# A two-layer spectral mixer with an MLP on one core: weight steps after every sequence product and on another engine, matrix loads at other calls, more places for second weights

## The chip, the cores and the metric

The kernel runs on one core of one Trainium2 chip. The metric is the device time of one execution in microseconds (us), lower is better. Before the change the median of 3 runs is 2772.48 us (2771.77 to 2774.47). TensorE (PE) multiplies, VectorE (DVE), ScalarE (ACT) and GpSimd (POOL) do elementwise work, and SyncE (SP) issues every DMA of this kernel, in the order of the program.

## The reference

The input is x of 2048 tokens by 576. Two layers run one after the other, and each is two residual steps, a Fourier mixing and an MLP:

```python
x = x + _A_ref(_layernorm(x), seq_re, seq_im, hid_re, hid_im)   # layer 1
x = x + _B_ref(_layernorm(x), w1, b1, w2, b2)
x = x + _A_ref(_layernorm(x), seq_re, seq_im, hid_re, hid_im)   # layer 2, same weights
x = x + _B_ref(_layernorm(x), w1, b1, w2, b2)

a = einsum("bsd,ed->bse", x, hid_re); b = einsum("bsd,ed->bse", x, hid_im)     # _A_ref
y = einsum("ts,bse->bte", seq_re, a) - einsum("ts,bse->bte", seq_im, b)
h = gelu(einsum("bsd,df->bsf", layernorm(x), w1) + b1)                          # _B_ref
y = einsum("bsf,fd->bsd", h, w2) + b2
```

The MLP's inner width is 4608. All data are 32-bit floats.

## The kernel before, in words

**Numbers in two parts.** Every matrix operand is kept as a high and a low part (the low part is the value minus its rounded high part), and each product is three passes, high by high, high by low, low by high. The high part is an ACT copy, the low part a subtraction. The products are arranged in a seven-product scheme (`ORDER` gives the order 1, 6, 2, 5, 7, 3, 4), so that sums and differences of operand blocks must be made as well.

**Stages.** The program runs, for each of the two layers: `Sequence.run` (products along the sequence, results to `uv_mid` in memory), then twice (half 0 and half 1 of the tokens) the function `hidden` (products with the hidden matrix, whose parts lie in `dh_parts`, and the normalization) with `mlp` behind it. I call the layers 1 and 2.

**The sequence.** After two first tiles, `run` (L602) goes through 14 tiles of 7 products. Each step makes the low part of the operand two products ahead on DVE (`low`, L556), the high part three ahead on ACT (`high`, L551), the 24 matmuls (`mms`) and the work on the result (`post`, L577). In `post` of product 7, ACT copies the bank, POOL adds (L593) and DVE combines (L594). Once per tile DVE makes two sums for the next tile (`sums`, L544), from blocks whose load is issued when a block of this tile comes free.

**The weight steps.** In layer 1 the first weights w1 must be split once for all later use. The generator `weights` (L247) does this in 126 steps, 7 for each of 18 groups. A step is: two ACT copies into a staging block (`high`, L265), later the subtraction (`low`, L270, at L275) and a store to `w1_parts`; in four steps of seven, POOL also makes the next operand (the `add` and `sub` of L251), and in four a block of raw weights is loaded. Each call of `pump` does one `low` and the next `high`. `run` calls it through `tick(3)`, three times in four products; the first products of the MLP (`inner`, L1003) call `tick(2)`, once in two products, and `load_w` calls it where a group is not made yet. After the 98 sequence products 73 pumps are done, and 55 more steps fall into the first MLP.

**The MLP.** `mlp` (L911) runs 18 times `inner` (7 products each with w1, results through gelu into hidden blocks), and behind each odd and even one a part of `outer` (L1098) for the pair of the step before: products 1, 6, 5, 3 behind the even one, 7, 4, 2 behind the odd. `outer` makes two calls of 12 matmuls for each product. Its second weights w2 come in slots `c2` of 4 x 288 elements: in half 0 two slots and a third that `give1` adds. In layer 1, half 0 (`first`), they are made on the way by `make` (L951): POOL differences, an ACT high part (L957), a DVE low part, and a store to `w2s`; a slot must have been stored before it is written again. In all later halves `load_w` loads them.

**Getting half 1 ready.** In the last `outer` of half 0 (g == 8, 14 calls) each call also does `next(after)`, a step of `Hidden.steps` (L685): it takes the place of Y, loads x, the sequence results `uv_mid` and the nine blocks of `dh_parts` (576 KB each), and turns the first tile on PE. All these loads and those of w2 go through SP's queue, in order.

Of the kernel before, what the change touches and what calls it, by code (L numbers as in the profile page):

```python
# [153 lines left out]
def spectral_mixer(ctx: ExitStack, tc: tile.TileContext, x, dh, c0, cs, w1, b1, w2, b2, out):  # L154
# [38 lines left out]
    def sub(engine, dst, a, b):  # L193
        engine.tensor_tensor(dst, a, b, op=OP.subtract)  # L194
# [46 lines left out]
        nc.scalar.activation(dst, src, AF.Identity, bias=mv[:, 4:5], scale=mv[:, 3:4])  # L241


    made = [0]
    stage, raw = R.alloc(3 * 5 * P, low=True), A.alloc(4 * 3 * P, low=True)

    def weights():  # L247
# [14 lines left out]
        def cut(a):  # L262
            return a.rearrange("p (k f) -> p k f", f=P)
# [6 lines left out]
        def low(n):  # L270

            q, k = divmod(n, 7)
            i, src, then = steps[k]
            t = cut(at(n))
            sub(nc.vector, t[:, 0:5:2], cut(src), t[:, 1:4].bitcast(F32))  # L275
            dma(w1s[q, i - 1], at(n).bitcast(F32))
            if then:
                then()
            if k in (2, 4, 5, 6):
                load(q + 1, (2, 4, 5, 6).index(k))  # L280
            if k == 6:
                made[0] = q + 1
# [32 lines left out]
    class Sequence:  # L315
# [286 lines left out]
        def run(self, hidden):  # L602
# [17 lines left out]
            for n, (t, i) in enumerate(steps):  # L620
                self.load_c()
                if n + 2 < len(steps):
                    self.low(*steps[n + 2])
                if i == 2 and t + 1 < NT:
                    self.sums(t + 1)
                self.load_c()
                if n + 3 < len(steps):
                    self.high(*steps[n + 3])
                self.mms(t, i)
                self.post(t, i)  # L630
                if t == NT - 1:
                    hidden.begin(self, ORDER.index(i))
                tick(3)
            for k in range(2):
                self.L[k].free()
            self.own.close()
# [5 lines left out]
    class Hidden:  # L642
# [41 lines left out]

        def steps(self):  # L685
            self.uvs = Slots(R, 2, 2 * D, Y_AT[0])
            self.X = A.place(X_AT[1], NT * DH)
            self.places = [R.place(Y_AT[0] + 4 * D + k * 2 * D, 2 * D) for k in range(KH)]

            def load_d(k):  # L690
                b = self.places[k].at
                self.load_d(k, Block(R, b, D), Block(R, b + D, D))

            self.load(0)
            load_d(0)
            yield
            self.load(1)
            load_d(1)
            for k in range(KH):
                yield  # L700
                if k + 2 < KH:
                    load_d(k + 2)
                self.high_d(k)
                if k:
                    self.low_d(k - 1)
            yield
            self.low_d(KH - 1)
            drain(self.turn(0, R.place(UT_AT[1][0], 2 * KH * P)))
            self.load_uv(2)
            yield  # L710
# [200 lines left out]
    def mlp(hid, store, first, after):  # L911
# [186 lines left out]
        def outer(g, i, side):  # L1098
            for jj in range(2):
# [14 lines left out]
                work(slot[0] % 3 < 2 or g >= last - 1)  # L1114
                slot[0] += 1
                advance()
                if g == last:
                    next(after, None)
                to = goal[i][:, 2 * jj:2 * jj + 2]
                if i == 6 and g == 0:  # L1120
# [24 lines left out]
        for g in range(NG + 1):  # L1145
            at[0] = 0
            if first and g:
                due.extend(make(g - 1))
            if g == NG:
                work(99)  # L1150
                c1.close()
                hs.close()
                Y.free()
            for f in range(2):
                if g < NG:
                    for _ in inner(2 * g + f, None if g or f else 1):
                        pass
                if g:
                    advance(6 + 15 * f)
                    at[0] = 7 + 15 * f  # L1160
                    slot[0] = 0
                    for i in OUTER[f]:
                        outer(g - 1, i, 1 - f)
# [81 lines left out]
```

## Time and profile before

| what | before |
|---|---|
| median of 3 runs | 2772.48 us |
| the profiled execution | 2771.1 us, of which its span is 2769.3 us |
| PE busy | 2684.4 us (97%) |
| DVE, ACT, POOL busy | 1756.6, 1087.4, 791.9 us |
| DMA moved | 543.74 MB, mean 196 GB/s |

The profile is of one execution. Its lists give, for an engine, the time that it stood idle and what ended that idle time; `A` and `R` are the two large on-chip buffers (plain, and rounded for matmul), `bank` is the accumulator memory, and `w_parts`, `dh_parts`, `uv_mid`, `x_mid` are tensors in memory. In a list by time the columns are start, length, engine, line, operation, operands, count, and in brackets the idle time before and what ended it. Lines 191 and 194 are the helpers `add` and `sub`, line 201 is `mm`, line 188 is `dma`, so a group is told apart by its operands and shape. By time, layer 1's sequence lies at about 12 to 376 us, its half 0 until 908, its half 1 until about 1390; layer 2's sequence until about 1770, half 0 until 2271, half 1 to the end.

### The profile page before, as it was taken

How to read it: one execution, taken by the hardware profiler on the slowest of the kernel's cores; microseconds unless marked ns; L12 is line 12 of the kernel's file. 1: busy time of each engine (PE TensorE's matmuls, PEld its weight loads, DVE VectorE, ACT ScalarE, POOL GpSimd, SP SyncE). 2: the span in 40 equal slices, each digit the busy share in tenths (PEclk: the TensorE clock that was granted, in tenths of full speed). 3: DMA queues.
4: the chain of work that ended last, by engine and by line, in shares of the span. 5: the costliest groups of instructions: out<-in, count | busy, mean ns of one | idle time of the engine just before them, and what ended most of it. 6: DMA issues, size and time to landing. Idle time of an engine off the chain costs nothing.

```text
span 2769.3 us, 45580 instructions
## 1 busy us (share of the span) xinstructions
PE 2684.4 (97%) x17596; PEld 2513.2 (91%) x17596; DVE 1756.6 (63%) x2566; ACT 1087.4 (39%) x1850; POOL 791.9 (29%) x762
## 2 busy tenths in 40 slices
PE   7999999999999999999989999999999999999999
PEld 7999998788888988989889999998999989998988
DVE  8788866777776465555577666555555544655555
ACT  6555544544443243333254333334333313433331
POOL 5222223544534332222251000042222224221222
PEclk9999999999999999999999999999999999999999
DMA  5666675777776546666553333526666663566664
GB/s 198 240 222 223 231 257 172 268 263 271 263 262 216 216 152 195 192 196 192 168 206 119 124 126 125 187 98 208 194 195 192 189 247 132 185 194 195 191 197 152
DMA packets 208712, 543.74 MB, mean 196 GB/s; under 512 B 21985, under 2 KB 56801, under 8 KB 208353
## 3 DMA queue, kind: packets, MB, share of 16 engines
q1 hardware_dynamic: 208496, 540.84, 58.7%
q8 instruction: 139, 2.28, 0.3%
q14 instruction: 77, 0.62, 0.1%
HBM read 428.69 MB, written 114.72 MB: 196 GB/s over the span
## 4 chain that ended last, share of the span: by engine, by line
PE 69%; DVE 5%; issue 3%; DMA 3%; POOL 2%; ACT 1%; SPq 0%; POOLq 0%; DVEq 0%; ACTq 0%
PE bank L201 68%; DVE R L194 2%; DMA R<-w_parts 1%; DVE A L191 1%; POOL A L194 1%; DMA A<-x_mid 1%; PE bank L764 1%; POOL R L194 1%; DMA w_parts<-R 0%; DVE bank L191 0%; DVE A L194 0%; DVE moments L216 0%; DVE moments L231 0%; ACT R L957 0%; ACT R L1073 0%
## 5 line engine op out<-in xcount | busy, mean ns | idle before, releaser
L201 PE MATMUL bank<-R 128*128 128x288 f32 (+2 forms) x16972 | 2624.9, 316 | 72.3 <-DVE A L191 23.3
L201 PEld LDWEIGHTS bank<-R 128*128 128x128 f32 x16972 | 2447.5, 189 | 240.9 <-DVE A L191 30.3
L191 DVE TENSOR_TENSOR A<-bank,A 128x576 f32<-128x576 f32 (+3 forms) x808 | 567.4, 710 | 613.5 <-PE bank L201 533.6
L194 POOL TENSOR_TENSOR R<-A,R 128x512 fp32r<-128x512 f32 x288 | 374.3, 1310 | 981.5 <-ACT R L1073 948.6
L194 DVE TENSOR_TENSOR R<-A,R 128x1024 fp32r<-128x1024 f32 (+4 forms) x449 | 447.3, 1024 | 44.7 <-ACT R L554 25.4
L191 POOL TENSOR_TENSOR A<-A 128x576 f32<-128x576 f32 (+2 forms) x102 | 131.1, 1287 | 639.0 <-ACT A L592 349.6
L1013 ACT ACTIVATE bank<-bank,b1t 128x512 f32<-128x512 f32 (+1 forms) x224 | 144.8, 646 | 373.8 <-DVE bank L191 253.6
L194 DVE TENSOR_TENSOR R<-bank,R 128x512 fp32r<-128x512 f32 (+4 forms) x408 | 251.6, 636 | 59.7 <-ACT R L197 50.2
L1073 ACT ACTIVATE R<-A 128x512 fp32r<-128x512 f32 x288 | 176.2, 628 | 276.4 <-DVE A L194 117.3
L554 ACT ACTIVATE R<-A 128x1024 fp32r<-128x1024 f32 x196 | 204.0, 1054 | 135.4 <-DVE A L194 105.5
L191 DVE TENSOR_TENSOR bank<-bank,A 128x512 f32<-128x512 f32 (+1 forms) x228 | 152.2, 670 | 152.1 <-PE bank L201 151.7
L194 POOL TENSOR_TENSOR A<-A 128x288 f32<-128x288 f32 (+2 forms) x170 | 200.6, 1193 | 154.9 <-DVE R L194 83.9
L197 ACT ACTIVATE R<-bank 128x512 fp32r<-128x512 f32 (+2 forms) x160 | 74.1, 514 | 185.6 <-PE bank L764 129.3
L1073 ACT ACTIVATE R<-bank 128x512 fp32r<-128x512 f32 x216 | 120.7, 595 | 32.0 <-PE bank L201 32.0
L194 DVE TENSOR_TENSOR A<-A 128x1024 f32<-128x1024 f32 (+2 forms) x116 | 127.7, 1106 | 4.3 <-ACT A L241 1.2
L1040 ACT ACTIVATE A<-bank 128x512 f32<-128x512 f32 (+1 forms) x76 | 43.7, 575 | 211.6 <-PE bank L201 208.9
L241 ACT ACTIVATE A<-A,moments 128x576 f32<-128x576 f32 x64 | 54.0, 868 | 113.0 <-POOL moments L224 80.7
L194 DVE TENSOR_TENSOR A<-bank,A 128x512 f32<-128x512 f32 x144 | 98.2, 682 | 0.0
L594 DVE SCALAR_TENSOR_TENSOR A<-A 128x288 f32<-128x288 f32 x28 | 18.4, 657 | 88.4 <-POOL A L191 88.4
L1013 ACT ACTIVATE A<-bank,b1t 128x512 f32<-128x512 f32 (+1 forms) x76 | 50.4, 663 | 54.8 <-DVE bank L191 54.8
L268 ACT ACTIVATE R<-A,power,middle 128x128 fp32r<-128x128 f32 x126 | 60.8, 483 | 0.0
L222 POOL TENSOR_TENSOR moments<-moments,power 128x1 f32<-128x1 f32 x32 | 17.6, 551 | 148.3 <-DVE moments L219 148.3
(50 smaller groups left out, 632.4 us busy)
## 6 DMA issues: line engine op xcount, KB each, us to landing
R<-w_parts SPq DMA_DIRECT2D x504, 320.0 KB, 3.3
R<-w_parts SPq DMA_DIRECT2D x189, 576.0 KB, 3.7
A<-in_cs SPq DMA_DIRECT2D x112, 512.0 KB, 4.3
w_parts<-R SPq DMA_DIRECT2D x126, 320.0 KB, 3.7
w_parts<-R SPq DMA_DIRECT2D x63, 576.0 KB, 4.0
uv_mid<-A SPq DMA_DIRECT2D x32, 576.0 KB, 2.8
A<-in_w SPq DMA_DIRECT2D x72, 192.0 KB, 3.8
R<-dh_parts SPq DMA_DIRECT2D x23, 576.0 KB, 10.5
```

The costliest lines, as they stand in the source:

```text
L191: engine.tensor_tensor(dst, a, b, op=op)
L194: engine.tensor_tensor(dst, a, b, op=OP.subtract)
L197: nc.scalar.activation(hi, src, AF.Copy)
L201: nc.tensor.matmul(o, a, b, start=start, stop=stop, skip_group_check=True)
L241: nc.scalar.activation(dst, src, AF.Identity, bias=mv[:, 4:5], scale=mv[:, 3:4])
L268: nc.scalar.activation(t[:, 2], src[:, 1], AF.Identity, bias=power[:, 2:3], scale=middle)
L554: nc.scalar.activation(self.cells[t, i](2, NP, P)[:, 0], self.source(t, i), AF.Copy)
L594: nc.vector.scalar_tensor_tensor(uv[:, 1, 0], p7, -1.0, u, op0=OP.mult, op1=OP.subtract)
L764: nc.tensor.transpose(at, v[:, k], ident)
L1013: nc.scalar.activation(dst, src, AF.Gelu_apprx_tanh, bias=bias(f))
L1040: nc.scalar.activation(up, o, AF.Copy)
L1073: nc.scalar.activation(H[q, k](2, TC)[:, 0], src, AF.Copy)
```

## The change

It has four edits.

1. `weights` subtracts on GpSimd while the first sequence runs, and on VectorE afterwards (`in_sequence`).
2. `run` pumps after every product, 98 times, in place of `tick(3)`.
3. `Hidden.steps` loads the nine matrix blocks one at each of its first nine steps and x behind them, and its steps begin six calls earlier, in `outer(7, ...)` of 7, 4, 2. For that Y and the w1 slots are freed behind the last `inner`, not at the next round.
4. In half 0, `c2` gets a place at R 0 as soon as that is free (in layer 1 when the weight steps are done), and behind the last `inner` two places where w1 lay.

```diff
-    made = [0]
+    made, in_sequence = [0], [True]
...
-            sub(nc.vector, t[:, 0:5:2], cut(src), t[:, 1:4].bitcast(F32))
+            sub(g if in_sequence[0] else nc.vector, t[:, 0:5:2], cut(src), t[:, 1:4].bitcast(F32))
...
-                tick(3)
+                pump()
+            in_sequence[0] = False
...
             self.uvs = Slots(R, 2, 2 * D, Y_AT[0])
-            self.X = A.place(X_AT[1], NT * DH)
             self.places = [R.place(Y_AT[0] + 4 * D + k * 2 * D, 2 * D) for k in range(KH)]
-
-            def load_d(k):
+            self.load_uv(0)
+            for k in range(KH):
                 b = self.places[k].at
                 self.load_d(k, Block(R, b, D), Block(R, b + D, D))
-
+                yield
+                if k == 2:
+                    self.load_uv(1)
+            self.X = A.place(X_AT[1], NT * DH)
             self.load(0)
-            load_d(0)
             yield
             self.load(1)
-            load_d(1)
-            for k in range(KH):
+            for _ in range(6):
                 yield
-                if k + 2 < KH:
-                    load_d(k + 2)
-                self.high_d(k)
-                if k:
-                    self.low_d(k - 1)
-            yield
-            self.low_d(KH - 1)
             drain(self.turn(0, R.place(UT_AT[1][0], 2 * KH * P)))
...
-                if g == last:
+                if g == last or half == 0 and g == last - 1 and side == 0:
                     next(after, None)
...
                 work(99)
-                c1.close()
                 hs.close()
-                Y.free()
+            if half == 0 and len(c2.idle) < 4:
+                more = R.place(0, 4 * DH)
+                if more:
+                    c2.idle.append(more)
...
+                if g == last and f:
+                    c1.close()
+                    Y.free()
+                    if half == 0:
+                        c2.idle += [R.place(C1_AT[0] + k * 4 * DH, 4 * DH) for k in range(2)]
```

**POOL in layer 1's sequence.** These are POOL's rows over one tile and a bit; 128x384 is the operand that a weight step makes, 128x288 is the addition of `post` of product 7. Before:

```order
L191 TENSOR_TENSOR A<-A 128x384
L191 TENSOR_TENSOR A<-A 128x288
L194 TENSOR_TENSOR A<-A 128x384 x3
L191 TENSOR_TENSOR A<-A 128x288
L191 TENSOR_TENSOR A<-A 128x384
```

With the change, where 128x3x128 is the subtraction of a weight step:

```order
L194 TENSOR_TENSOR R<-A,R 128x3x128 x4
L191 TENSOR_TENSOR A<-A 128x384
L194 TENSOR_TENSOR R<-A,R 128x3x128
L194 TENSOR_TENSOR A<-A 128x384
L191 TENSOR_TENSOR A<-A 128x288
L194 TENSOR_TENSOR R<-A,R 128x3x128
L194 TENSOR_TENSOR A<-A 128x384
L194 TENSOR_TENSOR R<-A,R 128x3x128
L194 TENSOR_TENSOR A<-A 128x384
```

Every tile now has seven subtractions, four operands and the addition on POOL, always in the same places: the subtraction of 7's pump stands right behind the addition that DVE waits for. On DVE the rows 128x3x128 are gone from the sequence, and 30 are left in the first MLP.

**SP at the end of half 0, layer 2.** These are the loads of SP's queue; 128x1152 from `w_parts` is one second weight (640 is a first weight, the last ones). Before, from the last first weights to the stores of the result:

```order
L188 DMA R<-w_parts 128x1152 x3
L188 DMA R<-uv_mid 128x1152
L188 DMA A<-x_mid 128x2x288
L188 DMA R<-dh_parts 128x1152
L188 DMA R<-uv_mid 128x1152
L188 DMA A<-x_mid 128x2x288
L188 DMA R<-dh_parts 128x1152
L188 DMA R<-w_parts 128x1152
L188 DMA R<-dh_parts 128x1152 x2
L188 DMA R<-w_parts 128x1152
L188 DMA R<-dh_parts 128x1152 x2
L188 DMA R<-w_parts 128x1152
```

With the change, from the same place:

```order
L188 DMA R<-w_parts 128x1152
L188 DMA R<-uv_mid 128x1152
L188 DMA R<-dh_parts 128x1152
L188 DMA R<-w_parts 128x1152
L188 DMA R<-dh_parts 128x1152
L188 DMA R<-w_parts 128x1152
L188 DMA R<-dh_parts 128x1152
L188 DMA R<-uv_mid 128x1152
L188 DMA R<-dh_parts 128x1152
L188 DMA R<-w_parts 128x1152
L188 DMA R<-dh_parts 128x1152 x2
L188 DMA R<-w_parts 128x1152
```

The second and third row of matrices now stand before second weights that were ahead of all of them, but the whole list begins with `outer(7, ...)` of 7, 4, 2, six calls earlier, and x has moved behind the matrices.

**SP at the end of half 0, layer 1.** Here the second weights are stored. Before:

```order
L188 DMA R<-dh_parts 128x1152 x2
L188 DMA w_parts<-R 128x1152
L188 DMA R<-dh_parts 128x1152 x3
L188 DMA w_parts<-R 128x1152
L188 DMA R<-dh_parts 128x1152 x2
L188 DMA w_parts<-R 128x1152 x2
```

With the change:

```order
L188 DMA R<-dh_parts 128x1152 x3
L188 DMA R<-uv_mid 128x1152
L188 DMA R<-dh_parts 128x1152 x3
L188 DMA w_parts<-R 128x1152 x2
L188 DMA R<-dh_parts 128x1152
L188 DMA w_parts<-R 128x1152
```

Six of the nine matrix loads have moved ahead of all seven stores of the last second weights.

## The prediction

> **What bounds the kernel now.** I read the page first, then busy time by stretch, then what PE waited for in each stretch, then the list by time around the longest waits, and last the groups of VectorE and GpSimd in the two sequences.
>
> ```profile
> span 2769.3 us, 45580 instructions
> PE 2684.4 (97%) x17596; PEld 2513.2 (91%) x17596; DVE 1756.6 (63%) x2566; ACT 1087.4 (39%) x1850; POOL 791.9 (29%) x762
> ```
>
> PE is the bound: 85 us are all that it stands idle, so each edit is worth what it gives back, or takes, there. The stretches are, from the top, layer 1's sequence, the end of its first MLP, its change from half 0 to half 1, layer 2's sequence, and layer 2's change to half 1.
>
> ```profile
> core 0: us, PE busy (x) PEld busy (x) DVE busy (x) ACT busy (x) POOL busy (x), PEclk, DMA share, GB/s
> 100.00:376.00 276.00, 276.00 (x2090) 276.00 (x2089) 229.49 (x251) 151.08 (x271) 67.87 (x49) 1.00 0.68 230
> 836.00:876.00 40.00, 38.94 (x235) 34.72 (x233) 27.82 (x41) 16.07 (x27) 15.67 (x12) 1.00 0.53 184
> 866.00:911.00 45.00, 36.38 (x238) 34.67 (x237) 26.05 (x36) 10.61 (x18) 18.33 (x13) 0.89 0.71 269
> 1500.00:1760.00 260.00, 260.00 (x1969) 260.00 (x1968) 169.66 (x177) 100.92 (x129) 9.71 (x12) 1.00 0.33 117
> 2246.00:2276.00 30.00, 24.10 (x169) 23.40 (x168) 11.15 (x16) 1.26 (x3) 8.98 (x7) 0.94 0.95 365
> ```
>
> In both sequences PE never stops, so there the change can only lose. At the two changes of half PE loses 8.6 of 45 us and 5.9 of 30 us, and the granted clock falls to 0.89 and 0.94: there it can win.
>
> **Layer 1's change of half (more places, earlier loads).** The list by time, SP's, ACT's, DVE's and PE's rows:
>
> ```profile
> 889.20 5.25 SPq L188 DMA_DIRECT2D R<-dh_parts  x3
> 895.54 0.32 SPq L188 DMA_DIRECT2D w_parts<-R  x1
> ...
> 900.63 0.68 ACT L957 ACTIVATE R<-A 128x576 fp32r<-128x576 f32 x1 [5.73 <-DMA w_parts<-R]
> 902.02 1.42 DVE L191 TENSOR_TENSOR A<-bank,A 128x576 f32<-128x576 f32 x2
> 902.91 5.22 PE L201 MATMUL bank<-R 128*128 128x288 f32 x24 [5.96 <-DVE A L191]
> ```
>
> Read it backwards. PE waits 5.96 us for DVE to empty a bank; DVE stood behind a low part; that behind ACT's copy, which waited 5.73 us until the store of a second weight had freed its slot; and the store stood in SP's queue behind matrix loads. With the change `c2` has six places by then (two, `give1`'s, R 0, and two of w1's; the steps are done long before, so R 0 is free), and seven weights are made: six copies find a free place, the seventh that of product 1, whose store is first of all. Six of the nine matrix loads leave the queue earlier, too. So the 5.96 us go. For the speed behind it:
>
> ```profile
> 2258.79 8.04 PE L201 MATMUL bank<-R 128*128 128x288 f32 x48 [4.17 <-DMA R<-w_parts]
> 2267.93 3.44 PE L201 MATMUL bank<-R 128*128 128x288 f32 x24 [1.11 <-DMA R<-w_parts]
> 2272.20 1.86 PE L201 MATMUL bank<-R 128*128 128x288 f32 x12
> ```
>
> 24 matmuls take 3.44 us at full clock and took 5.22 behind the wait, 1.78 more. Together **-7.7**. The short waits at the head of this `outer` (its first weight is made just before it is used) I leave, for their order does not change.
>
> **Layer 2's change of half.** The same rows show its price: 4.17 and 1.11 us of waiting for second weights, and 48 matmuls in 8.04 us where 3.44 + 2 x 1.58 = 6.60 would do (1.58 is 3.44 less 1.86), 1.44. Together 6.7. The weights stood behind matrix loads in a queue that moved 365 GB/s at a share of 0.95. With the change the queue begins six calls, some 6 x 1.6 = 9.6 us, earlier, and one more weight is there when it begins. From there it carries six weights and nine matrices of 0.59 MB, two of `uv_mid` of the same size, and x, 10.6 MB. The last weight is the 16th piece: 9.4 MB / 365 GB/s = 26 us. It is used at the 19th call, 18 x 1.6 = 29 us on; the one before it is the 13th, 21 us, and used at 26. Both come in time by 3 to 5 us, so **-6.7**.
>
> **The first MLP (fewer steps in it).** What PE waited for, first from 676 to 836 us, then from 836 to 876, after the last weight step:
>
> ```profile
> PE bank L201 <- DVE bank L191: 3.3, 4, 0.8
> PE bank L201 <- DVE A L191: 1.8, 3, 0.6
> PE bank L201 <- DMA R<-w_parts: 1.3, 2, 0.7
> ...
> PE bank L201 <- DVE A L191: 1.0, 1, 1.0
> ```
>
> With steps going on, there is a wait in each `inner` (six, 4.6 us; DVE comes late to a bank that the last product needs) and one in each second `outer` (three, 1.8 us). Without them only the one in `outer` is left, with 1.0 us. Now 30 steps are left for this MLP, one in two products, so 60 products, 8.6 of 18 `inner`: they end near 676 us, as I count the `inner` in PE's rows. From there to 836, 6.4 us become 3 x 1.0: **-3.4**. Before 676 the steps stand at the same products as they did, so nothing.
>
> **Layer 1's sequence (a step per product, subtracted by GpSimd).** Groups of DVE and POOL, first from 100 to 376 us, then of DVE in layer 2's stretch, where no step runs; the last number before the idle time is the mean in ns:
>
> ```profile
> L194 DVE TENSOR_TENSOR R<-A,R 128x1024 fp32r<-128x1024 f32 x87 | 111.5, 1284 | 6.1 <-ACT R L554 6.0
> L194 DVE TENSOR_TENSOR A<-A 128x1024 f32<-128x1024 f32 x36 | 48.3, 1341 | 1.2
> L194 DVE TENSOR_TENSOR R<-A,R 128x384 fp32r<-128x384 f32 x65 | 39.5, 608 | 0.6 <-issue 0.6
> L594 DVE SCALAR_TENSOR_TENSOR A<-A 128x288 f32<-128x288 f32 x13 | 10.7, 825 | 26.7 <-POOL A L191 26.7
> L194 POOL TENSOR_TENSOR A<-A 128x384 f32<-128x384 f32 x27 | 40.0, 1480 | 57.7 <-DVE R L194 30.1 <-issue 23.0 <-DMA A<-in_w 4.1
> L191 POOL TENSOR_TENSOR A<-A 128x384 f32<-128x384 f32 x9 | 17.2, 1910 | 97.7 <-DVE R L194 97.7
> ...
> L194 DVE TENSOR_TENSOR R<-A,R 128x1024 fp32r<-128x1024 f32 x82 | 98.9, 1219 | 9.8 <-ACT R L554 9.8
> L594 DVE SCALAR_TENSOR_TENSOR A<-A 128x288 f32<-128x288 f32 x12 | 5.5, 459 | 54.3 <-POOL A L191 54.3
> ```
>
> The same DVE operation is longer where POOL works: 1284 against 1219 ns, 825 against 459. The list by time shows why:
>
> ```profile
> 152.73 1.00 POOL L194 TENSOR_TENSOR A<-A 128x384 f32<-128x384 f32 x1
> 157.88 1.02 POOL L194 TENSOR_TENSOR A<-A 128x384 f32<-128x384 f32 x1 [4.15 <-issue]
> ...
> 152.80 1.25 DVE L594 SCALAR_TENSOR_TENSOR A<-A 128x288 f32<-128x288 f32 x1 [2.06 <-POOL A L191]
> 155.69 1.22 DVE L194 TENSOR_TENSOR A<-A 128x1024 f32<-128x1024 f32 x1
> 157.20 0.55 DVE L194 TENSOR_TENSOR R<-A,R 128x384 fp32r<-128x384 f32 x1
> 158.10 1.88 DVE L194 TENSOR_TENSOR R<-A,R 128x1024 fp32r<-128x1024 f32 x1 [0.35 <-ACT R L554]
> ```
>
> A DVE operation on two on-chip operands that meets a POOL operation ends only when POOL has ended and its own work is done: 1.88 in place of 1.22, 1.25 in place of 0.46. One meeting costs DVE 0.66 to 0.79 us. So what leaves DVE comes back as hold-up. The sum over these 276 us (12.4 tiles of 22.2 us): DVE without steps takes 169.66 / 260 x 276 = 180. Before, 229.5: 65 subtractions of 0.55 are 36, the other 13 are hold-up by 49 POOL operations. After: no subtractions, but 87 of them and 50 operand steps (four in seven) on POOL, 137 operations of 1.00 us beside the 13 additions. At the hold-up of before (13.5 / 49 = 0.28 each) DVE comes to 180 + 38 = 218, and nothing is lost. If each meets DVE, it comes to 180 + 137 x 0.66 = 270, or with 0.79 to 288: 6 below the 276 or 12 above, over 14 tiles nothing or 14 us. I take the row of 0.66, since DVE works nearly without a break then and nearly each meets it; its 6 us are 0.5 us a tile, and the waits that DVE cannot fill (0.35 for ACT above, and the 2.06 where 7's pump now puts a subtraction right behind the addition) take some more than that, an estimate of 0.3 us a tile: **+4**, between 0 and 14.
>
> The other parts cost nothing I can name: ACT has 25 steps of two short copies more, in a stretch where it is busy 151 of 276 us; SP's queue has 25 stores more and the share of the DMA is 0.68; but SP now waits for POOL before it issues a store, and matrix loads for the next tile's sums stand behind it. That is in the 14 us.
>
> On this the Trainium skill has a rule: "SBUF — State Buffer", section "SBUF: two separate sides", says that VectorE operations with two SBUF inputs and GpSimd share a port pair as an exclusive lock, held for the whole instruction. The rows agree in kind (an operation is held up, not slowed), and by 0.66 to 0.79 us, not by the whole 1.00. The skill's "GPSIMD Engine Reference", section "4.1 Engine selection", advises against GpSimd for elementwise work; taken alone, it would make the subtraction 1.00 for 0.55 us and change nothing while PE bounds.
>
> **The sum.** 2769.3 - 7.7 - 6.7 - 3.4 + 4 = 2755.5 us of span. The profiled execution took 2771.1, 1.8 more than its span, and the median 2772.48, 1.4 above that: 2755.5 + 1.8 + 1.4 = **2758.7**.
>
> **Rivals.**
> - *VectorE and GpSimd take turns all through layer 1's sequence, and bound it* (slower). Each of 137 operations would hold DVE up for its whole 1.00 us: 180 + 137 = 317 for 276, over 14 tiles (311 us) +46 in place of +4: 2801. It costs anything from (276 - 180) / 137 = 0.70 us of hold-up on, and the kernel is slower by over 0.2% from 0.86 on. For it speaks that POOL's mean is already 1480 and 1910 ns, waiting its own turn; against it that no quoted DVE operation was held 0.86. Up to 0.86 the gain is only eaten: 2764 to 2778. The skill's lock, held for the whole instruction, would make this 2801.
> - *The loads are late anyway* (layer 2). If the queue moved 300 GB/s, the last weight would land at 31 us, 2 us after its use; with the slower clock behind the wait some 4 of the 6.7 us stay: 2763. For it: four weights and six matrices are now issued in under 10 us.
> - *The stall of layer 1 isn't the slot's.* If ACT's copy would wait for the difference that POOL makes for it as long as for the slot, the 7.7 us stay: 2766. Against it: its row names the store.
>
> **How the numbers follow.** The forecast 0.62 (own range 2752 to 2764); gains eaten by hold-up 0.20; slower by it 0.08; late loads or the stall staying 0.10. The range 2750 to 2776 leaves out the slow end and gains beyond those counted. A run can tell 0.2%, 5.5 us, from no change. Faster by more than that (under 2767): 0.62, most of the last case, and a little of the second, 0.74; within, 0.18; slower, 0.08.
>
> **What would show it.** Right: PE's waits from 676 us on without those of `inner`; no wait over 2 us at either change of half, and the clock near 1 there; in layer 1's sequence PE busy nearly throughout, DVE near 270 of 276 us, its 1024-wide subtraction at a mean of 1.5 to 1.9 us. Wrong: PE idle in layer 1's sequence, ended by DVE, of more than 1 us a tile; or waits for `w_parts` left in layer 2.

## The result, and the profile after

The changed kernel takes 2773.89 us (median of 12 runs, 2770.63 to 2776.7), the kernel before on the same chips 2771.89 (12 runs, 2769.98 to 2774.47): a ratio of 1.0008, interval 1.0000 to 1.0015. No difference that can be told, where I forecast 2758.7.

The page's head, the counterpart of the two lines of before:

```profile
span 2773.3 us, 45524 instructions
...
PE 2689.5 (97%) x17596; PEld 2513.7 (91%) x17596; DVE 1766.4 (64%) x2470; ACT 1085.8 (39%) x1850; POOL 954.4 (34%) x858
```

PE has the same 17596 matmuls and idles 83.8 us (2773.3 - 2689.5) where it idled 84.9: nothing seems to have happened. Cut at marks that both traces have, it is a large gain and a large loss. The marks are the first transposes of `turn` (L764 before, L758 now) of a layer, and the first 256-wide matmul of an MLP:

| stretch of PE's rows, us | before | after | difference | forecast |
|---|---|---|---|---|
| start to layer 1's first transposes | 376.6 | 395.1 | **+18.5** | +4 |
| on to its first MLP | 80.0 | 85.8 | **+5.8** | 0 |
| on to the MLP of its half 1 | 531.9 | 517.5 | **-14.4** | -7.7 - 3.4 |
| on to layer 2's first transposes | 788.5 | 790.0 | +1.5 | 0 |
| on to the MLP of its half 1 | 574.8 | 567.5 | **-7.3** | -6.7 |
| on to the last matmul | 410.8 | 410.7 | -0.1 | 0 |
| sum | 2762.6 | 2766.6 | +4.0 | -13.8 |

The sum is the difference of the two spans, 2773.3 - 2769.3. The first MLP and the ends of the halves gave 21.7 us, more than the 17.8 forecast; layer 1's sequence and what follows it took 24.3. The +1.5 arises where layer 2's sequence begins: between 1380 and 1500 us PE's longest wait is 7.3 us where it was 5.9; why was not followed.

**The ends of the halves.** Busy time by stretch, after, with the same columns as before: layer 1's sequence, layer 1's change of half, layer 2's.

```profile
100.00:376.00 276.00, 268.30 (x1977) 262.46 (x1976) 246.13 (x176) 152.33 (x291) 219.73 (x143) 1.00 0.72 245
...
875.00:920.00 45.00, 40.81 (x260) 37.62 (x259) 30.49 (x43) 13.47 (x23) 17.82 (x13) 0.96 0.87 321
2250.00:2281.00 31.00, 30.29 (x228) 29.78 (x228) 18.02 (x28) 3.79 (x7) 13.71 (x10) 1.00 0.81 318
```

At the changes of half the clock is 0.96 and 1.00 where it was 0.89 and 0.94. What PE waited for, in us, times and longest, before, first from 836 to 911 us, then from 2225 to 2285:

```profile
PE bank L201 <- DVE A L191: 7.6, 4, 6.0
...
PE bank L201 <- DMA R<-w_parts: 5.3, 2, 4.2
```

And after: from 100 to 376, from 376 to 481, from 700 to 855 (the stretch that was 676 to 836), from 855 to 920, and from 2225 to 2290 us:

```profile
PE bank L201 <- DVE R L194: 6.8, 17, 0.7
...
PE bank L201 <- DVE R L194: 6.3, 4, 4.5
...
PE bank L201 <- DMA R<-w_parts: 0.3, 1, 0.3
...
PE bank L201 <- DVE A L191: 3.4, 5, 1.0
...
PE bank L201 <- DVE A L191: 0.7, 1, 0.7
```

The wait of 6.0 us is gone (1.0 is left in its place), and so are the 5.3 for second weights in layer 2. Where layer 1's half 0 got its 14.4 us (14.5 before rounding) shorter is seen by comparing the n-th matmul of PE after with the n-th before. The changed kernel is 24.4 us late at the first matmul of the first MLP, 23.6 late at the matmul that before has at 676 us, 16.6 at 836 and 16.5 at 895, 11.5 behind the long wait, and 9.8 from 920 us on. So the first MLP gave 7.9 us, 7.0 of them from 676 us on (6.1 are waits: 0.3 where 6.4 had been), and the change of half 6.7: 5.0 by the wait, 1.7 by the matmuls behind it, which ran at a higher clock.

**Layer 1's sequence.** PE, busy for all 276.00 us before, is busy for 268.30, in 1977 matmuls where 2090 were done. The waits are small, 17 of at most 0.7 us in this list, and these are all for a DVE low part. The count says more than the busy time: at 276 / 2090 = 0.132 us each, the 113 matmuls that are missing are 14.9 us, while the rows book 7.7 as idle; the rest is in PE rows that have grown longer. A tile takes 23.63 us on the mean where it took 22.21. POOL and DVE by groups in the same stretch, in the form of the prediction's; the first row is POOL's addition before, the others are after:

```profile
L191 POOL TENSOR_TENSOR A<-A 128x288 f32<-128x288 f32 x13 | 11.0, 844 | 51.6 <-ACT A L592 51.6
...
L194 POOL TENSOR_TENSOR R<-A,R 128x384 fp32r<-128x384 f32 x83 | 121.7, 1466 | 54.2 <-ACT R L268 50.5 <-POOL R L194 3.7
L194 POOL TENSOR_TENSOR A<-A 128x384 f32<-128x384 f32 x36 | 61.2, 1700 | 0.9
...
L191 POOL TENSOR_TENSOR A<-A 128x288 f32<-128x288 f32 x12 | 20.6, 1718 | 0.5
...
L194 DVE TENSOR_TENSOR R<-A,R 128x1024 fp32r<-128x1024 f32 x82 | 147.1, 1805 | 8.9 <-ACT R L554 8.4
L194 DVE TENSOR_TENSOR A<-A 128x1024 f32<-128x1024 f32 x36 | 60.8, 1690 | 1.2
```

DVE is as forecast in kind (1805 and 1690 ns for its large operations), and busy for 246 us, not 270: it idles 30 us of 276. POOL is the news: the addition for product 7 has a mean of 1718 ns where it had 844. DVE, ACT and POOL over one tile, chosen from the list by time:

```profile
254.28 1.26 DVE L594 SCALAR_TENSOR_TENSOR A<-A 128x288 f32<-128x288 f32 x1 [0.70 <-POOL A L191]
...
260.57 1.23 DVE L194 TENSOR_TENSOR R<-A,R 128x1024 fp32r<-128x1024 f32 x1 [0.76 <-ACT R L554]
...
263.78 1.92 DVE L194 TENSOR_TENSOR A<-A 128x1024 f32<-128x1024 f32 x1
...
263.07 0.89 SPq L188 DMA_DIRECT2D A<-in_w  x1
265.74 0.33 SPq L188 DMA_DIRECT2D A<-in_cs  x1
266.16 0.38 SPq L188 DMA_DIRECT2D w_parts<-R  x1
266.60 0.43 SPq L188 DMA_DIRECT2D A<-in_w  x1
...
271.64 0.42 ACT L267 ACTIVATE R<-A 128x256 fp32r<-128x256 f32 x1 [2.96 <-DMA A<-in_w]
...
275.23 0.39 ACT L592 ACTIVATE A<-bank 128x288 f32<-128x288 f32 x1
...
272.52 1.19 POOL L194 TENSOR_TENSOR R<-A,R 128x384 fp32r<-128x384 f32 x1 [2.03 <-ACT R L268]
273.68 1.99 POOL L194 TENSOR_TENSOR A<-A 128x384 f32<-128x384 f32 x1
275.70 1.71 POOL L191 TENSOR_TENSOR A<-A 128x288 f32<-128x288 f32 x1
...
277.44 1.25 DVE L594 SCALAR_TENSOR_TENSOR A<-A 128x288 f32<-128x288 f32 x1 [0.70 <-POOL A L191]
```

This is a closed loop, and its turn, 277.44 - 254.28 = 23.16 us, is the tile. DVE combines product 7's result, and comes to the block subtraction that ends at 265.70; SP, which goes by the order of the program, issues nothing from 263.96 until then, when its load of `in_cs` may overwrite that block, and behind it stand a store and the load of a raw weight block, issued at 266.60; ACT stands at the copy of it until 271.64; POOL then does that step's subtraction and operand, 1.19 and 1.99 us, and only behind them the addition for product 7, 1.71 us; then DVE combines again. DVE takes 11.4 us of the turn, SP 0.9, the load 5.0, ACT 0.9 and POOL 4.9. Two lines end at the addition almost together: POOL's operand at 275.67, and ACT's copy of product 7's result (L592), which ACT comes to only behind the weight copies, at 275.62. So by these rows, taking either one away alone would gain little.

### The profile page after: what moved, and what is told of

It reads as the page before. It is cut to its first block, busy times and chain, and to the rows that moved or that the text cites. A ratio compares the mean times of both kernels' runs of the same rounds, so it can differ in the third digit from the quotient of the medians.

```text
span 2773.3 us, 45524 instructions
## 1 busy us (share of the span) xinstructions
PE 2689.5 (97%) x17596; PEld 2513.7 (91%) x17596; DVE 1766.4 (64%) x2470; ACT 1085.8 (39%) x1850; POOL 954.4 (34%) x858
## 4 chain that ended last, share of the span: by engine, by line
PE 73%; DVE 3%; DMA 2%; issue 2%; POOL 1%; ACT 1%; SPq 0%; POOLq 0%; DVEq 0%; ACTq 0%
PE bank L201 72%; DVE R L194 1%; DMA R<-w_parts 1%; POOL A L194 1%; PE bank L758 1%; DVE A L191 1%; POOL R L194 0%; DMA A<-in_cs 0%; DMA w_parts<-R 0%; DMA A<-x_mid 0%; DVE moments L216 0%; DVE A L194 0%; PE bank L828 0%; DVE moments L231 0%; ACT R L483 0%
## 5 line engine op out<-in xcount | busy, mean ns | idle before, releaser
L194 POOL TENSOR_TENSOR R<-A,R 128x512 fp32r<-128x512 f32 (+1 forms) x384 | 519.2, 1361 | 1120.1 <-ACT R L1067 998.1
L194 DVE TENSOR_TENSOR R<-A,R 128x1024 fp32r<-128x1024 f32 (+5 forms) x353 | 430.8, 1239 | 46.2 <-ACT R L554 31.5
L191 POOL TENSOR_TENSOR A<-A 128x576 f32<-128x576 f32 (+2 forms) x102 | 144.5, 1419 | 380.9 <-ACT A L592 298.9
L194 POOL TENSOR_TENSOR A<-A 128x288 f32<-128x288 f32 (+2 forms) x170 | 207.1, 1226 | 107.3 <-DVE R L194 53.1
L194 DVE TENSOR_TENSOR A<-A 128x1024 f32<-128x1024 f32 (+2 forms) x116 | 141.6, 1226 | 4.3 <-ACT A L241 1.3
L267 ACT ACTIVATE R<-A 128x256 fp32r<-128x256 f32 x126 | 51.5, 409 | 64.9 <-DMA A<-in_w 49.2
L594 DVE SCALAR_TENSOR_TENSOR A<-A 128x288 f32<-128x288 f32 x28 | 24.0, 856 | 73.7 <-POOL A L191 73.7
```

The source lines that it names most:

```text
L191: engine.tensor_tensor(dst, a, b, op=op)
L267: nc.scalar.activation(t[:, 1:4:2], src[:, 0:3:2], AF.Copy)
L594: nc.vector.scalar_tensor_tensor(uv[:, 1, 0], p7, -1.0, u, op0=OP.mult, op1=OP.subtract)
```

## Experiments

Each table gives layer 1's first transposes (where the sequence ends), the mean of the 12 tiles behind the first, and the time with its ratio to the kernel before on the same chip. A tile is taken from one copy of product 7's result on ACT to the next.

### One edit at a time

a1 undoes edit 1, a2 edit 2, a3 both (all with the diff's lines), a4 undoes edits 3 and 4, so that only the steps are left.

```diff
 a1: -            sub(g if in_sequence[0] else nc.vector, t[:, 0:5:2], ...
     +            sub(nc.vector, t[:, 0:5:2], ...
 a2: -                pump()
     +                tick(3)
```

> Edit 1 undone: every weight subtraction on VectorE, still a step per product. Theory H (GpSimd's operations hold VectorE up on the chain from product 7 to the low part of the next tile's product 6): 82 subtractions of 0.55 us return to VectorE and 82 hold-ups go; the first hidden product of layer 1 begins near 377 us as before the change (395 with it), tiles of 22.2 us, and the span is 2773.3 less 15 to 22: 2751 to 2758. Rival R (the step rate: two more ACT copies, a store and waits of SP's queue per product): the tiles stay at 23 us or more and the span at 2768 to 2774.

> Edit 2 undone: three steps in four products, subtracted by GpSimd. H: 103 GpSimd operations in place of 142 hold VectorE up, tiles of 22.3 to 22.9 us, so 2 to 10 us of the sequence's 24 stay lost; in the first MLP 55 steps stand again, 3 to 6 us back: span 2757 to 2767. R: tiles of 22.2 us, no loss in the sequence: span 2753 to 2757.

> Edits 1 and 2 undone: only the loads, the earlier steps and the places for second weights. Both theories: the sequence as before the change, the two changes of half as with it (7.7 and 7.3 us less than before), the first MLP's steps as before: span 2753 to 2756. If part of the first MLP's gain comes from the fourth place and not from fewer steps, down to 2750.

> Edits 3 and 4 undone: only GpSimd's subtraction and a step per product. Both theories: the sequence's 24 us lost and 3 to 7 us won in the first MLP, the waits at the changes of half as before: span 2786 to 2792. If the last tile of the sequence loses its 6 us through something that the loads at the ends set off, less than that.

| kernel | subtraction | steps in a tile | transposes at | tile | us | ratio (interval) |
|---|---|---|---|---|---|---|
| before | DVE | 5.25 | 376.6 | 22.21 | | |
| after | POOL | 7 | 395.1 | 23.63 | 2773.89 | 1.0008 (1.0000 to 1.0015) |
| a1 | DVE | 7 | 394.8 | 23.54 | 2777.90 | 1.0012 (1.0003 to 1.0022) |
| a2 | POOL | 5.25 | 378.2 | 22.31 | 2763.52 | 0.9962 (0.9947 to 0.9977) |
| a3 | DVE | 5.25 | 376.6 | 22.21 | 2759.17 | 0.9950 (0.9934 to 0.9967) |
| a4 | POOL | 7 | 394.2 | 23.53 | 2789.38 | 1.0055 (1.0040 to 1.0070) |

The gain of the ends (a3) and the loss of the steps (a4) stand apart: edits 3 and 4 alone give 0.5%, a span of 2757.3 us, a little less gain than the 2753 to 2756 that I expected. The steps are not a sum of two costs: the fourth step in four costs 18.2 us with DVE subtracting and 16.9 with POOL, and POOL's subtraction costs 1.6 with three steps in four and nothing with all. So hold-up of DVE by POOL, on which my forecast rested, can't be the whole: a1 takes POOL's 96 subtractions in the sequence away and loses the same.

### Where the wait is, and where it goes

In a1 ACT waited for raw weights too (19.2 us from 100 to 376), as in the change (37.3). So I tried the group's last three steps in the order 6, 7, 3, which reloads the late block earlier (b1 as the change, b2 with DVE), no reload in the sequence at all (b3), and no steps in the last tile (b4).

```diff
 b1: -                 (7, a21, None), (6, a11, None), (3, a12, None))
     +                 (6, a11, None), (7, a21, None), (3, a12, None))
     ...
     -                load(q + 1, (2, 4, 5, 6).index(k))
     +                load(q + 1, {2: 0, 4: 2, 5: 1, 6: 3}[k])
 b3: -            if k in (2, 4, 5, 6):
     +            if k in (2, 4, 5, 6) and not in_sequence[0]:
 b4:                  if t == NT - 1:
                          hidden.begin(self, ORDER.index(i))
     -                pump()
     +                else:
     +                    pump()
```

> The changed kernel with the last three steps of a weight group in the order 6, 7, 3 in place of 7, 6, 3, so that the raw block a11 is loaded again one step earlier, four pumps before ACT copies it in place of two. Theory W (with a step per product a weight group takes one tile, and ACT, in order, stands before the copy of a raw block that has not landed; the operand copies of the sequence stand behind it): ACT's waits for in_w (37 us from 100 to 376 us) fall under 10, tiles go from 23.5 to 22.2 to 22.7 us, the span from 2773 to 2756 to 2764. Rival H (GpSimd's and VectorE's operations holding each other up): tiles stay at 23.2 us or more, span 2769 to 2774.

> The same order 6, 7, 3 with the subtraction on VectorE. W: tiles 22.2 to 22.4 us, the first hidden product of layer 1 near 378 to 380 us (395 without the order), and with the first MLP's gain a span of 2750 to 2756, the lowest so far. H: as it was, 2772 to 2776.

> The changed kernel that does not load raw weight blocks again while the first sequence runs (the weights that it makes there are not those of the reference; all other work is done). W: no wait for in_w is left, tiles 22.2 to 22.8 us, first hidden product near 377 to 385 us. H: tiles of 23.2 us or more, 393 to 396 us.

> The changed kernel without steps in the last tile of the first sequence (7 fewer there, 7 more in the MLP). If the 6 us that are lost between the first hidden product and the first MLP (85.8 us with the change, 80.0 before) come from steps beside the hidden matrix parts, that stretch is back at 80 to 81 us and the span 4 to 6 us lower, 2767 to 2770; if they come from the lateness of the sequence before, it stays at 84 to 86 us.

| kernel | transposes at | tile | us | ratio (interval) |
|---|---|---|---|---|
| b1 | 399.8 | 24.03 | 2786.95 | 1.0050 (1.0033 to 1.0067) |
| b2 | 397.0 | 23.71 | 2778.55 | 1.0013 (1.0003 to 1.0022) |
| b3 | 391.4 | 23.28 | 2773.43 | 0.9992 (0.9982 to 1.0003) |
| b4 | 394.3 | 23.37 | 2771.02 | 0.9988 (0.9978 to 0.9999) |

In b1 ACT no longer waits for the load, POOL does (33.3 us), and ACT for the staging block's store (39.9): the wait moved and grew. In b3 no load is left to wait for, and only 3.7 of 18.5 us come back. SP's and ACT's rows in b3, over the same part of a tile, show what takes its place:

```profile
262.64 0.33 SPq L188 DMA_DIRECT2D A<-in_cs  x1
263.06 0.86 SPq L188 DMA_DIRECT2D w_parts<-R  x2
...
267.66 0.42 ACT L267 ACTIVATE R<-A 128x256 fp32r<-128x256 f32 x1 [2.08 <-DMA w_parts<-R]
```

The loop closes as before, through the store of a staging block in place of the load: it stands behind the same load of `in_cs`, and ACT's weight copy waits until it has freed the block. From one combination of DVE to the next it is 23.17 us here. The load is a link of the loop, not its cause. Of the expectations the second come nearer, though none is hit whole: b1's span is 2780.4 us (2769 to 2774), b2's 2779.4 (2772 to 2776), and b3's transposes come at 391.4 (393 to 396). b4 settles the second loss: from the transposes to the MLP it takes 79.4 us, as before (80.0), where the change takes 85.8. In the change the steps of the last tile stood there beside DVE's low parts of the hidden matrix, and PE waited once for 4.5 us.

### Two loops?

From these I took it that there were two loops, one through product 7's result, too long only with POOL, and one through the load, each enough by itself. c1 removes both (DVE, no reload); c2 slows the rate (DVE, no step behind product 7); c3 keeps POOL but takes the step at product 7 ahead of that product's result, without reloads; the fourth shortens POOL's subtraction to 8 of 128 columns.

```diff
 c2: -                pump()
     +                if i != 7:
     +                    pump()
 c3: +                if i == 7:
     +                    pump()
                      self.post(t, i)
     ...
     -                pump()
     +                if i != 7:
     +                    pump()
 b3_small_sub:
     -            sub(g if in_sequence[0] else nc.vector, t[:, 0:5:2], cut(src), t[:, 1:4].bitcast(F32))
     +            sub(g if in_sequence[0] else nc.vector, t[:, 0:5:2, :8 if in_sequence[0] else P], ...
```

> The change with the weight subtraction on VectorE and without the loads of further raw weights in layer 1's sequence (this leaves out those loads, so from the second group on the weights are not those of the reference). Theory of two loops: with one step per product there are two loops that are each longer than the 22.2 us of a tile: (1) product 7's result through ACT, GpSimd's addition, VectorE and ACT to the low part of the next tile's product 6, too long only with GpSimd's subtractions in it; (2) the seven weight steps of a group, with ACT standing at a weight copy for the load that was issued behind the last use of its block. Here both are gone: tiles of 22.2 to 22.5 us, first hidden product at 376 to 381 us, span 2756 to 2762. Rival, too much work on VectorE (seven more subtractions of 0.55 us and their waits a tile): tiles stay at 23.0 and more, first hidden product at 389 to 396.

> The change with the subtraction on VectorE and six steps in a tile: none behind product 7. A group of seven steps then has 8.17 products, 25.9 us, in place of 22.2. Theory of two loops: the loop of the group fits, the other one is short with VectorE's subtraction: tiles of 22.2 to 22.5 us, first hidden product at 376 to 381; 84 of 126 steps are done in the sequence, so the first MLP gets some 11/25 of the 9.8 us that it gained with 98: in all 2751 to 2758, the fastest so far. Rival, work on VectorE: the loss goes with the number of steps, 11/25 of 18 us, so first hidden product near 384 and in all 2760 to 2766.

> The change, GpSimd subtracting, with product 7's weight step ahead of the work on product 7's result, and without the loads of further raw weights in layer 1's sequence (so the weights are not the reference's from the second group on). Theory of two loops: the second loop is gone as in the run without these loads; of the first, 10.4 us there where some 10.0 may be, one subtraction of 1.0 us and VectorE's turn behind it are taken out from between GpSimd's addition and VectorE: tiles of 22.2 to 22.7, first hidden product at 377 to 384. Rival, GpSimd's hold-up of VectorE alone, whatever the order: as without the move, tiles near 23.1 and first hidden product at 389 to 393.

> The change with GpSimd subtracting only 8 of each block's 128 columns in layer 1's sequence (this leaves out most of the low parts of those weights). GpSimd's subtraction gets short and VectorE has none. Theory of two loops: the first loop is short again, the second still has its load to wait for, begun somewhat earlier: tiles of 22.3 to 23.2, first hidden product at 380 to 392, with ACT still waiting for the raw weights. Rival, hold-up alone: the 98 subtractions were 98 of the 137 more GpSimd operations, so less than a third of the loss is left, first hidden product at 376 to 382 and no wait of PE over 0.3 us a tile.

| kernel | transposes at | tile | us | ratio (interval) |
|---|---|---|---|---|
| c1 | 384.9 | 22.75 | 2761.94 | 0.9960 (0.9945 to 0.9976) |
| c2 | 377.3 | 22.21 | 2761.98 | 0.9960 (0.9946 to 0.9974) |
| c3 | 407.2 | 24.54 | 2788.74 | 1.0054 (1.0034 to 1.0074) |
| b3_small_sub | 377.3 | 22.21 | 2753.38 | 0.9927 (0.9907 to 0.9947) |

The theory fell in three of four, and in the fourth, c2, the sequence came as expected but the time, 2761.98, lies above the 2751 to 2758. c1 came between the two expectations; c3 got worse by 15.8 us than without its move; and a short POOL subtraction gave the whole tile back, with the load still made. c3 has its reason in the code: a step ahead of `post` puts its two ACT copies ahead of product 7's copy and its subtraction and operand ahead of POOL's addition, so, as I read it, it made longer what I wanted shorter. b3_small_sub says that with POOL it is the length of POOL's operations, on POOL's own line or by what they hold DVE up (DVE is busy 206 us of 276, for 246); it does not part these two. What c1 still waited for is in ACT's list by time:

```profile
245.05 0.42 ACT L267 ACTIVATE R<-A 128x256 fp32r<-128x256 f32 x1 [2.16 <-POOL A L191]
...
246.71 0.39 ACT L592 ACTIVATE A<-bank 128x288 f32<-128x288 f32 x1
```

The copy of product 7's result (L592) has no wait of its own: the bank was full long before, but ACT does things in order, and stood at a weight copy until POOL had made that step's operand. That is one particular step. With seven steps in a tile the same step of the group meets product 7 every time; with 5.25 or six, each in turn. Place was a candidate beside rate.

### Place or rate

d1 and d2 keep seven steps a tile and begin them four products later, so that the steps without an operand stand at products 5, 7 and 3; d4 two products later (n >= 2); d1 and d3 subtract on POOL, d2 and d4 on DVE; d3 is the change with c2's edit, six steps.

```diff
 d1: -                pump()
     +                if n >= 4:
     +                    pump()
```

> The change as it is, GpSimd subtracting, but with its steps begun four products later (94 in the sequence in place of 98). Seven steps a tile, as in the change; only another step of the group meets product 7: the steps without an operand for GpSimd to make stand at products 5, 7 and 3, and those with one at 4, 1, 6 and 2. Theory of place: the loss is one chain, from the raw block's load through ACT's weight copy, GpSimd's subtraction and operand at product 5's step, its addition for product 7, VectorE, ACT and VectorE to the low part of the next product 6; without the operand of 2.0 us and the wait for the load in it, it fits: tiles of 22.2 to 22.7 us, first hidden product at 376 to 383, in all 2753 to 2763. Rival, rate: seven steps do not fit in 22.2 us wherever they stand: tiles of 22.9 and more, first hidden product at 388 to 396.

> The same four products' shift with the subtraction on VectorE. Theory of place: the same chain, shorter still: tiles of 22.2 to 22.4 us, first hidden product at 376 to 380, in all 2751 to 2758, the fastest with seven steps a tile. Rival, rate: as without the shift, tiles of 22.9 and more, first hidden product at 386 to 395.

> The change, GpSimd subtracting, with six steps in a tile (none behind product 7), so that each step of the group meets each product in turn. Theory of place: only in some tiles does an operand stand ahead of the addition for product 7: tiles of 22.2 to 23.0, first hidden product at 379 to 386, in all 2755 to 2764. Rival, hold-up by the number of GpSimd's operations: 84 + 48 of the change's 98 + 56, so most of the loss of 18.5 us stays, first hidden product at 388 to 394.

> The subtraction on VectorE, the steps begun two products later (96 in the sequence). The operand of the group's first step is then made behind product 7's addition and the step without operand stands at product 5. Theory of place: ACT's weight copy at product 5 waits for no operand, though the load it needs is issued two steps ahead as ever: tiles of 22.2 to 22.8, first hidden product at 376 to 385. Rival, rate: as without the shift, first hidden product at 388 to 395.

| kernel | subtraction | transposes at | tile | us | ratio (interval) |
|---|---|---|---|---|---|
| d1 | POOL | 397.6 | 24.10 | 2778.28 | 1.0017 (1.0008 to 1.0027) |
| d2 | DVE | 375.7 | **22.21** | **2754.92** | 0.9933 (0.9918 to 0.9948) |
| d3 | POOL | 386.4 | 22.90 | 2771.90 | 0.9995 (0.9985 to 1.0005) |
| d4 | DVE | 375.9 | 22.21 | 2755.07 | 0.9934 (0.9914 to 0.9954) |

**With DVE it is place.** d2 has a step behind every product, as a1 has, and loses nothing, and neither does d4 with another shift. The shift moves whole steps, their loads and stores too, so the runs show the place of the step; which of its parts matters is read from rows. a1's list by time over one tile, some rows of POOL, ACT and DVE:

```profile
271.63 1.93 POOL L191 TENSOR_TENSOR A<-A 128x384 f32<-128x384 f32 x1 [12.81 <-DVE R L194]
...
275.71 0.89 POOL L191 TENSOR_TENSOR A<-A 128x288 f32<-128x288 f32 x1 [0.86 <-ACT A L592]
...
273.59 0.42 ACT L267 ACTIVATE R<-A 128x256 fp32r<-128x256 f32 x1 [1.59 <-POOL A L191]
...
275.25 0.39 ACT L592 ACTIVATE A<-bank 128x288 f32<-128x288 f32 x1
...
276.63 1.26 DVE L594 SCALAR_TENSOR_TENSOR A<-A 128x288 f32<-128x288 f32 x1 [0.70 <-POOL A L191]
...
281.87 1.94 DVE L194 TENSOR_TENSOR R<-A,R 128x1024 fp32r<-128x1024 f32 x1 [0.29 <-ACT R L554]
```

What PE waited for in a1, from 100 to 376 us:

```profile
PE bank L201 <- DVE R L194: 8.7, 11, 0.9
```

And d2's ACT at the same products:

```profile
258.77 0.41 ACT L267 ACTIVATE R<-A 128x256 fp32r<-128x256 f32 x1
...
261.64 0.41 ACT L592 ACTIVATE A<-bank 128x288 f32<-128x288 f32 x1 [1.12 <-PE bank L201]
```

In a1 the chain runs operand, weight copy, product 7's copy (which waits for nothing), addition, combination, and DVE's low part that PE waits for, once a tile. In d2 the weight copy ahead of L592 waits for nothing, and L592 itself waits 1.12 us for PE: ACT is ahead again.

**With POOL the shift does not help.** d1 has the same places as d2, and one of the longest tiles of all, 24.10 us where the change has 23.63. d1's list by time, POOL over a tile, then DVE and ACT, then POOL again:

```profile
212.31 1.30 POOL L194 TENSOR_TENSOR R<-A,R 128x384 fp32r<-128x384 f32 x1 [4.26 <-DMA A<-in_w]
213.69 1.88 POOL L191 TENSOR_TENSOR A<-A 128x384 f32<-128x384 f32 x1
215.53 2.00 POOL L194 TENSOR_TENSOR R<-A,R 128x384 fp32r<-128x384 f32 x1
217.49 2.01 POOL L194 TENSOR_TENSOR A<-A 128x384 f32<-128x384 f32 x1
219.46 1.99 POOL L194 TENSOR_TENSOR R<-A,R 128x384 fp32r<-128x384 f32 x1
221.41 2.00 POOL L194 TENSOR_TENSOR A<-A 128x384 f32<-128x384 f32 x1
...
229.23 0.81 POOL L191 TENSOR_TENSOR A<-A 128x288 f32<-128x288 f32 x1
...
216.57 2.04 DVE L194 TENSOR_TENSOR R<-A,R 128x1024 fp32r<-128x1024 f32 x1
...
220.50 2.03 DVE L191 TENSOR_TENSOR A<-A 128x1024 f32<-128x1024 f32 x1
...
230.07 1.25 DVE L594 SCALAR_TENSOR_TENSOR A<-A 128x288 f32<-128x288 f32 x1 [1.68 <-POOL A L191]
231.25 2.04 DVE L194 TENSOR_TENSOR R<-A,R 128x1024 fp32r<-128x1024 f32 x1
233.32 1.22 DVE L194 TENSOR_TENSOR A<-A 128x1024 f32<-128x1024 f32 x1
...
234.58 1.06 ACT L554 ACTIVATE R<-A 128x1024 fp32r<-128x1024 f32 x1 [5.12 <-DVE A L194]
235.54 0.40 ACT L267 ACTIVATE R<-A 128x256 fp32r<-128x256 f32 x1
...
236.46 1.30 POOL L194 TENSOR_TENSOR R<-A,R 128x384 fp32r<-128x384 f32 x1 [4.26 <-ACT R L268]
```

POOL goes from 212.31 to 230.04 with hardly a break, ten operations, and those in the middle begin every 1.96 us (215.53, 217.49, 219.46, 221.41). An operation that took 1.00 us alone takes 2.00, for DVE's 1024-wide ones stand between: one of each in 1.96 us, where DVE's takes 1.22 by itself. They take turns, and POOL loses by it (1.00 us an operation) as DVE does (0.8). Product 7's addition stands behind nine of them; DVE, ACT's copies and the next step's subtraction then follow in line, and the turn is 236.46 - 212.31 = 24.15 us.

d3, with six steps, came between its two expectations: the tile, 22.90 us, is within the first, the time, 2771.90, far above its 2755 to 2764. The loss goes with the number of operations that POOL has in a tile: a2 has 9.25 (5.25 subtractions, 3 operands, 1 addition) and tiles of 22.31 us, d3 10.4 and 22.90, and the kernels with 12 have 23.28 (b3) to 24.54 (c3). It is not POOL's sum that sets the tile. At 1.96 us each, 12 operations would be 23.5 us, more than the 22.21 of PE's work; but not all of them meet DVE's large ones, and POOL is busy 219.73 us of the change's 276, 80%. What sets the tile, as far as the rows show it, is the closed loops, in which POOL's operations stand in line with DVE's, ACT's and a transfer.

**The version that beats both** is d2: the changed kernel with the subtraction left on DVE and its steps begun four products later, 2754.92 us, 0.9933 of before (d4, 2755.07, can't be told from it).

## Why the prediction was wrong

- **Layer 2's change of half, -6.7: right.** Measured -7.3; the 5.3 us for `w_parts` are gone and the clock is 1.00.
- **Layer 1's change of half, -7.7: right.** Matmul by matmul it gave 6.7. The mechanism is the forecast one: the wait of 5.96 us is gone but for 1.0, which I had not kept, and the matmuls behind it are 1.7 us faster, where I put 1.78.
- **The first MLP, -3.4: right in kind, too small.** From 676 us on it gave 7.0. The waits with steps going on went from 6.4 to 0.3 us, 6.1. I kept 1.0 us for each of three parts of `outer`, taken from the one wait that before has behind its last step; from 700 to 855 none of them came.
- **Layer 1's sequence, +4 (0 to 14): wrong, and the step that failed.** Measured +18.5, and +5.8 behind it. It was put as "nearly each meets it; its 6 us are 0.5 us a tile", with "an estimate of 0.3 us a tile" for what the waits that DVE cannot fill take beyond these. I counted the time that POOL takes from DVE, and asked if DVE's sum still fits into 276 us. It did: 246 us. Even the price of a meeting was near: against DVE's time without steps, an estimate from 169.66 us in 260 of layer 2 and tiles of 23.63, DVE was held up some 0.6 us by each of 131 POOL operations, where I took 0.66. What was wrong is the path. The tile is not set by the sum of an engine but by the line in which things stand: product 7's addition behind a subtraction and an operand on POOL, which is held up as well (its mean is 1718 ns for 844), and product 7's copy behind weight copies on ACT, which wait for a load or a store. The turn of that line is 23.16 us in the rows above, 0.95 more than the 22.21 of PE's work. The second error is a term put at nothing: "The other parts cost nothing I can name", because ACT is busy 151 of 276 us. a1, without any subtraction on POOL, loses 18.2 us by the step per product alone. Seven steps against seven products fix which step stands at product 7, for all tiles.
- **The rivals.** "VectorE and GpSimd take turns all through layer 1's sequence" names what lengthens the change's loop, with the wrong bound, and a1 loses the same without it. For it I had quoted POOL's means of 1480 and 1910 ns as "waiting its own turn", and put the limit where DVE would be full. Its lower case, gains "only eaten", 2764 to 2778, holds the result, but by a sum of hold-up that was not what cost the time; that is luck. Neither late loads in layer 2 nor a stall that is not the slot's came true.
- **The edit that I thought harmless.** I argued the place of 7's pump only with POOL's cost. a1 shows that the step per product costs as much on DVE, and d2 that starting four products later wins it back: 23 us of the median (2777.90 to 2754.92), 0.8% by the ratios.

On the rule of the Trainium skill that I weighed ("SBUF — State Buffer", section "SBUF: two separate sides"): it says that whichever of the two engines starts first gets the port pair, and the other is blocked. d1's rows agree, for both engines are blocked in turn; by the whole durations a pair would take 1.22 + 1.00 = 2.22 us, and it takes 1.96. So by the measurement some 0.26 us of each pair overlap.

What stays open: a1's first transposes come 18.2 us late and c1's 8.3, so some 10 of it hangs on the reloads, by the load of the raw block that ACT waits for or by the loads of `in_cs` behind it in SP's queue; no run parts these. That the tile of the change is set by the loop above is read from its rows. The run that cuts one link of it (b3) leaves a loop of the same length through another link; only the runs that slow the rate (a2) or shorten POOL's subtraction (b3_small_sub) bring the tile to 22.31 and 22.21. Neither of the two other places that were tried with POOL (c3 and d1) does.

## What to carry to other kernels

Before work is moved to an idle engine, write down for a tile all operations that this engine then has, each at the length it has when it meets the engine it shares with, and see which of its neighbours' results stands behind them in its order; a share of 25% busy (POOL's 67.87 of 276 us) says nothing on that. Where background steps are put between the main ones, mind the ratio: at one to one the same step meets the same place every time, and shifting the start by a few may be worth more than the rate. And take a change of several edits apart before judging it: two of these four gave 0.5% and the others took it back.

## What the runs showed of the hardware

A GpSimd operation on two on-chip operands of 384 columns took 1.00 us alone and 2.00 us between DVE's of 1024 columns, which in turn took 1.92 to 2.04 for 1.22; GpSimd then began one operation every 1.96 us (d1). With only 24 columns (b3_small_sub) the GpSimd operation took 0.24 to 1.22 us, and DVE had 206 us of work in 276 where it had 246. PE's clock was lower around waits of 1 us as well: 0.96 in the 45 us of the changed kernel's change of half, whose longest wait is 1.0.
